# Where deferred steps are issued in a fused attention and MLP kernel: from a slot's due list to its late list

## The chip, the cores and the metric

The kernel runs on one core of one Trainium2 chip. A core has a matrix engine (PE, with its weight loads PEld), a vector engine (DVE), a scalar engine (ACT), a general engine (POOL) and a queue engine (SP) that issues the transfers. The metric is the device time of one execution in microseconds (us). The time before is 510.4 us, the median of three runs (510.28 to 510.7).

## The reference

The input is x of 2048 rows by 512. Everything is in 32-bit floats. `ln` is a layer norm without weights.

```python
qkv = ln(x) @ wqkv                      # 32 heads of 16
idx = pos[:, None] - 2 * arange(8)      # each row sees 8 rows, two apart, backwards
attn = softmax(where(idx >= 0, (q . k[idx]) * 16 ** -0.5, -1e9))
h   = x + (sum over the 8 of attn * v[idx]) @ wo
r   = max(ln(h) @ w1 + b1, 0)           # 1792 wide
out = h + (r * r) @ w2 + b2
```

## The kernel before, in words

Matrix products run on operands that are split in a high part, which the matrix engine's fast 32-bit format holds exactly, and a low part, the rest. Each product is the sum of three terms (high by high, low by high, high by low). In the code `hi` is the cast that makes the high part (ACT, L152) and `lo` the subtraction that makes the low part (L155, on DVE or POOL as the caller says). The matrix product of the attention result with `wo`, of the normalised rows with `w1` and of the squared relu with `w2` are all made so.

The 16 row tiles of 128 rows are worked on in four groups of four. A first phase does the projections to q, k and v, which go to HBM (`qkv_d`) and come back in windows. Then come three passes, u = 0, 1 and 2, and a last one in another form. A pass u does the MLP of group u and, beside it, the attention and the product with `wo` of group u + 1. The passes have 17 slots: in each, PE does one block of 128 of the first product (`mlp1`, tile `mm`), and three slots later that block's second product (`mlp2`, into four tiles `acc`). Two slots hold each a `wo` product (tile `wo`), put in by `wo_product`.

The other engines get their work from lists, in an order set by the code alone; each engine then runs its own queue in that order, and an instruction that waits holds all that stands behind it on its engine. `at(n, f)` puts a step on the due list of the slot n from now, `midway` on a middle list, `after` on a late list. A slot ends with `end_slot`, which first issues the due list, then moves the attention on with `pump`, then issues the middle list and the late list. So a step from the due list stands ahead of the attention steps of its slot on each engine, and one from the late list behind them.

`pump` draws from the stream `attention`: DVE makes the products of q and k (`pr`, L339), sums them (L373), takes maximum and difference (`mx` L390, `ex` L392), then ACT makes the exponential (`ex`, L396), DVE sums (`sm`, L362), normalises (L379, L367) and multiplies with v (`pr`, L350); POOL adds up these products in a triplet of additions to the attention result `o` (L407). ACT also copies q in (`qp`, L268). SP loads the windows k and v (L247) and q (L260) as their buffers come free of DVE's last use.

What the change touches:

- Attention result t is split into 16-bit halves by ACT (`o_split`: `pl<-o`, L616), turned by a transposing transfer on SP (`turn_dma`, L620), joined by ACT (`o_join`, L625), and cast to the two parts `oh`/`ol` or `ohl`, which the `wo` product reads. The same goes for normalised rows `hn`. The index i counts a group's four results; RI is 2.
- After a `wo` product come four steps: `h_add` (DVE, L661, with statistics L163 and L164, followed by three small steps `rs` of POOL), `h_norm` (ACT, `hn`, L196), `add_b2` (POOL, `h<-h,b_sb`, L674) and `spill` (SP to `h_d`, L677). `add_b2` prepares the row for the end of its own group's MLP.
- `split_w2` (u = 0 alone) makes the parts of one block of `w2` from `raw`: a cast into `big_h` or `w_x` at once, and a `lo` on the late list, on DVE for every third block and on POOL for the others. Low parts go to HBM (L1082) and are fetched in later passes (L1087).
- `hidden`, one slot after `mlp1`, makes relu and square on ACT (`r`, L871 and L872), the cast `rh` and, a slot later, the `lo` named `rl` on POOL.

The last pass works on pairs of blocks; POOL and DVE make sums of weights there (`traw`, L786 to L789), which ACT casts to `th` and a `lo` completes as `tl`.

Of the kernel before, what the change touches and what calls it, by code (L numbers as in the profile page):

```python
# [20 lines left out]
RI = 2  # L21
# [37 lines left out]
def block_kernel(ctx, tc, x, wqkv, wo, w1, b1, w2, b2, out):  # L59
# [53 lines left out]
    def at(delta, fn, *a):  # L113
        due.setdefault(now["slot"] + delta, []).append((fn, a))

    def after(delta, fn, *a):
        late.setdefault(now["slot"] + delta, []).append((fn, a))
# [4 lines left out]
    def end_slot(pe):  # L122
        now["pe"] += pe
        run(due)
        pump()
        run(amid)
        run(late)
        now["slot"] += 1

    def run(chores):  # L130
        todo = chores.get(now["slot"], [])
        while todo:
            fn, a = todo.pop(0)
            fn(*a)

    def dve(t):
        now["dve"] += t
# [80 lines left out]
    def mm3(ps, lh, ll, rh, rl, mid=None, at_=2 * KB, lows_last=False):  # L218


        terms = [[(l, r, k) for k in range(KB)] for l, r in ((lh, rh), (ll, rh), (lh, rl))]
        if lows_last:
            terms[1:] = terms[:0:-1]
        terms = sum(terms, [])
        for n, (l, r, k) in enumerate(terms):
            if mid and n == at_:
                mid()
            nc.tensor.matmul(ps, l(k), r(k), start=(n == 0), stop=(n == 3 * KB - 1))  # L228
# [454 lines left out]
    def wo_product(t, slots):  # L683
        ps = turn["mm"].tile("wo")
        oh, ol = oT.pop(t)
        mm3(ps, lambda k: oh[:, k, :], lambda k: ol[:, k, :],
            lambda k: wo_h[:, k, :], lambda k: wo_l[:, k, :], lows_last=t in OV)
        for n, (fn, a) in zip(slots, ((h_add, (t, ps)), (h_norm, (t,)), (add_b2, (t,)),
                                      (spill, (t,)))):
            (after if fn in (h_norm, spill) else at)(n + (fn is add_b2), fn, *a)  # L690

# [183 lines left out]
    def mlp1(u, f):  # L877
        ps = turn["mm"].tile("mm")
        fs = slice(f * P, (f + 1) * P)
        mm3(ps, lambda k: w1_h[:, k, fs], lambda k: w1_l[:, k, fs],  # L880
            lambda k: hh[k // 2][:, k % 2], lambda k: hl[k // 2][:, k % 2])
        at(1, hidden, u, f, ps)

    def mlp2(u, f, acc, js, first=False, last=False, mid=None):

        rh, rl = hid[u, f]
        terms = [(rh, w2_h, j) for j in js] + [(rh, w2_l, j) for j in js]
        if len(js) > 1:
            terms += [(rl, w2_h, j) for j in js]
        else:  # L890
            terms.insert(1, (rl, w2_h, js[0]))
        for n, (l, w, j) in enumerate(terms):
            if mid and n == len(terms) // 2:
                mid()
            nc.tensor.matmul(acc[j], l[:, j * P:(j + 1) * P], w[f],  # L895
                             start=(first and n < len(js)),
                             stop=(last and n >= len(terms) - len(js)))
# [79 lines left out]
    for n in range(16):  # L977
        gp, t = divmod(n, 4)
# [28 lines left out]
    def first_phase(t0):  # L1007
        def chores(m):
# [16 lines left out]
            for t in range(R):  # L1025
                if k == OT[t]:
                    at(0, load_h, t)
                    o_T(t)
                if t in HV and k == HK[t][0]:
                    at(0, h_split, t)  # L1030
                    after(0, turn_dma, ("h", t))
                if t in HV and k == HK[t][1]:
                    at(0, turn_join, ("h", t))
                if k == WO[t]:
                    wo_product(t, (1, 3, 4, 6))
                    now["pe"] += 2.73
                if k == HT[t]:
                    (at(0, h_parts, t) if t in HV else h_T(t))
# [12 lines left out]
    def load_w2(f):  # L1051
        raws[f] = row("raw2")
        nc.sync.dma_start(raws[f], w2[f * P:(f + 1) * P, :])
# [36 lines left out]
    for u in range(R - 1):  # L1090
        now["sub"] = u
        first, end = u == 0, False
        fs = list(range(FB)) if first else [*sorted(place), 12, 13]
        fs += [f for f in range(12) if f not in fs and (u < 2 or f not in ENDS)]
        fs += ENDS if u == 2 else []
        need = [] if first else [f for f in fs if f < 12 and f not in place]
        acc = [psum.tile([P, D], F32, name="acc", tag=tag) for tag in ("acc0", "acc1", "tr0", "tr1")]
        js = range(R)


        todo, halves = {}, {}
        for i in js:
            t = R * (u + 1) + i
            if not end:
                a = i // 2 if u == 2 else 0
                o0 = OP[i] - a - (2 if i >= RI and t in OV else 0)
                if t in OV:
                    turned = [(o0, at, 0, o_split, t), (o0, at if i >= RI else after, i // RI, turn_dma, ("o", t)),
                              (o0 + 2, at, 0, o_join, t)]
                else:  # L1110
                    turned = [(o0, o_T, t)]
                if t in HV:
                    h0 = 11 + i
                    turned += [(h0, midway, 0, h_split, t), (h0, after, 0, turn_dma, ("h", t)),
                               (h0 + 2, at, 0, turn_join, ("h", t))]
                for p, *what in ((LH[i] - a, at, 0, load_h, t), *turned,
                                 (WP[i] - a, wo_product, t, (0, 1, 2 + 3 * a, 3 + 3 * a))):
                    todo.setdefault(p, []).append(what)
                p, h = (HP[i], i % 2) if u < 2 else HL[i]
                if t in HV:  # L1120
                    todo.setdefault(p, []).append((at, 0, h_parts, t))
                else:
                    (todo, halves)[h].setdefault(p, []).append((h_T, t))
            todo.setdefault(UP[i], []).append((at, 0, unspill, R * u + i))
        if u == 2:
            for p, *what in ((12, at, 0, t_load, 0), (12, at, 0, t_load, 1), (13, after, 0, t_sums, 0),
                             (13, after, 0, t_sums, 1), (13, at, 1, t_split, 0),
                             (14, after, 0, t_split, 1)):
                todo.setdefault(p, []).append(what)

        def half(p):
            run(due)
            for fn, *a in halves[p]:
                fn(*a)

        for p in range(FB + LAG):
            more = 0.0
            if p == FB:
                run(due)
                dve(HOLD)  # L1140
            if u < 2 and p == FB - 2:
                dve(HOLD)
            for fn, *a in sorted(todo.get(p, []), key=lambda x: x[0] is wo_product):
                fn(*a)
                more += 2.73 if fn is wo_product else 0.0
            if p < FB:
                mlp1(u, fs[p])
                more += 2.73
                if first:
                    at(0, split_w2, p)  # L1150
                    if p + 1 < FB:
                        load_w2(p + 1)
            q = p - LAG
            if q >= 0:
                f = fs[q]
                mlp2(u, f, acc, js, q == 0, q == FB - 1,
                     (lambda: half(p)) if p in halves else None)
                more += 2.74
                if f < 12 and (need or first and p < FB - LAG):
                    free.append(place.pop(f))  # L1160
                    if need:
                        at(1, fetch, need.pop(0))
            end_slot(more)
        for i in js:
            at(u // 2, finish, R * u + i, acc[i])
# [83 lines left out]
```

## Time and profile before

| | |
|---|---|
| median of the runs | 510.4 us |
| the profiled execution | 510.82 us |
| its span | 509.0 us |
| PE busy | 498.7 us, 98% |
| DVE, POOL, ACT busy | 75%, 70%, 60% |
| granted clock of PE | 1.00 |

The span is the time between the first and the last recorded event of the profiled execution; the 1.8 us around it belong to its own time as well. A row of a timeline gives the start, the duration, the engine, the line, the operation, the tiles written and read (without their numbers), the shapes, how many instructions the row stands for, and in brackets how long the engine was idle before and whose event ended that. Matrix instructions overlap their neighbours, so that the distance between starts says more than the durations. In a row by stretches, each engine has its busy time and its count.

### The profile page before, as it was taken

To read this page: it belongs to the slowest core of one execution; us is meant where nothing else is said; L and a number is where in the kernel's file an instruction comes from. 1 tells how busy PE (TensorE), PEld (TensorE's weight loads), DVE (VectorE), ACT (ScalarE), POOL (GpSimd) and SP (SyncE) were. 2 spreads that over 40 slices of the span, in tenths; PEclk is the share of its full clock that TensorE was granted. 3 is DMA by queue.
4 is the path that set the end of the run, shared out by engine and by line. 5 is a ranking of instruction groups with operands and counts; after the bars stand their busy time and mean duration, and the time that the engine had idled before them with its cause. 6 is when DMAs were issued, how large, how long until landed. Compare 5 with 4: busy or idle time off the path is not lost.

```text
span 509.0 us, 7539 instructions
## 1 busy us (share of the span) xinstructions
PE 498.7 (98%) x2422; PEld 420.7 (83%) x2422; DVE 380.8 (75%) x512; ACT 304.7 (60%) x558; POOL 357.2 (70%) x434
## 2 busy tenths in 40 slices
PE   8999999999999999999999999989999999999997
PEld 7999778888888888887788888768888888998986
DVE  6469899999989799979879997898973137832233
ACT  4625677768346757386564566754556947566541
POOL 5714689986685899969777876976897465685610
PEclk9999999999999999999999999999999999999999
DMA  8577899989798898669676874967662372444212
GB/s 265 162 238 204 229 300 297 262 271 317 219 220 254 277 283 253 231 176 245 193 249 199 215 195 130 263 221 231 210 160 67 102 217 82 166 127 142 64 42 82
DMA packets 109359, 102.61 MB, mean 202 GB/s; under 512 B 29448, under 2 KB 77832, under 8 KB 109320
## 3 DMA queue, kind: packets, MB, share of 16 engines
q1 hardware_dynamic: 108376, 101.61, 68.0%
q10 hardware_dynamic: 944, 0.52, 0.3%
q8 instruction: 19, 0.31, 0.3%
q14 instruction: 20, 0.16, 0.1%
HBM read 72.65 MB, written 24.25 MB: 190 GB/s over the span
## 4 chain that ended last, share of the span: by engine, by line
PE 41%; POOL 5%; ACT 4%; DMA 3%; DVE 1%; issue 1%; SPq 0%; POOLq 0%; DVEq 0%; ACTq 0%
PE acc L895 19%; PE mm L228 12%; PE mm L818 6%; PE wo L228 3%; POOL pr L407 2%; DMA o<-pl 1%; DMA hn<-pl 1%; POOL h L674 1%; DMA h<-h_d 1%; ACT pl L625 1%; ACT pl L616 1%; ACT hn L196 1%; DVE pr L350 0%; POOL o L407 0%; PE tr L201 0%
## 5 line engine op out<-in xcount | busy, mean ns | idle before, releaser
L407 POOL TENSOR_TENSOR pr<-pr 128x512 f32<-128x512 f32 (+1 forms) x128 | 133.7, 1044 | 34.6 <-DVE pr L350 29.1
L228 PE MATMUL mm<-big_l,w_h 128*128 128x512 f32 x336 | 88.5, 390 | 1.6 <-DVE big_l L155 0.9
L350 DVE TENSOR_TENSOR pr<-ex,v 128x1024 f32<-128x1024 f32 x64 | 78.1, 1221 | 13.1 <-POOL o L407 8.1
L339 DVE TENSOR_TENSOR pr<-qp,k 128x1024 f32<-128x1024 f32 x64 | 76.8, 1200 | 8.8 <-ACT qp L268 6.9
L373 DVE TENSOR_REDUCE ex<-pr 128x64 f32<-128x1024 f32 x64 | 78.5, 1226 | 1.9
L228 PEld LDWEIGHTS mm<-big_l,w_h 128*128 128x128 f32 x336 | 62.9, 188 | 15.4 <-issue 1.3
L155 POOL TENSOR_TENSOR rl<-r,rh 128x512 fp32r<-128x512 f32 x42 | 55.5, 1322 | 20.2 <-ACT rh L152 20.2
L228 PE MATMUL mm<-big_l,xh 128*128 128x512 f32 (+1 forms) x208 | 55.8, 378 | 0.0
L228 PE MATMUL mm<-big_h,xh 128*128 128x512 f32 (+1 forms) x208 | 53.9, 380 | 1.3 <-ACT xh L152 1.0
L228 PE MATMUL mm<-big_h,xl 128*128 128x512 f32 (+1 forms) x208 | 52.7, 375 | 0.7 <-DVE xl L155 0.7
L895 PE MATMUL acc<-big_l,rh 128*128 128x512 f32 x190 | 52.2, 390 | 0.0
L895 PE MATMUL acc<-big_h,rh 128*128 128x512 f32 x190 | 52.1, 391 | 0.0
L895 PE MATMUL acc<-big_h,rl 128*128 128x512 f32 x190 | 51.7, 389 | 0.0
L228 PEld LDWEIGHTS mm<-big_h,xh 128*128 128x128 f32 x208 | 37.6, 188 | 8.9 <-ACT xh L152 2.6
L228 PE MATMUL mm<-big_l,w_l 128*128 128x512 f32 x168 | 44.9, 389 | 0.0
L228 PEld LDWEIGHTS mm<-big_h,xl 128*128 128x128 f32 x208 | 38.2, 188 | 6.9 <-DVE xl L155 1.1
L871 ACT ACTIVATE r<-mm,b_sb 128x512 f32<-128x512 f32 x42 | 28.7, 684 | 22.5 <-PE mm L228 20.7
L895 PEld LDWEIGHTS acc<-big_h,rl 128*128 128x128 f32 x190 | 35.7, 188 | 7.4
L895 PEld LDWEIGHTS acc<-big_l,rh 128*128 128x128 f32 x190 | 35.5, 188 | 7.4
L228 PEld LDWEIGHTS mm<-big_l,xh 128*128 128x128 f32 x208 | 37.5, 188 | 4.9
L895 PEld LDWEIGHTS acc<-big_h,rh 128*128 128x128 f32 x190 | 34.9, 188 | 6.7
L228 PEld LDWEIGHTS mm<-big_l,w_l 128*128 128x128 f32 x168 | 31.5, 188 | 6.6
(167 smaller groups left out, 918.7 us busy)
## 6 DMA issues: line engine op xcount, KB each, us to landing
k<-qkv_d SPq DMA_DIRECT2D x48, 288.0 KB, 3.0
v<-qkv_d SPq DMA_DIRECT2D x48, 288.0 KB, 4.1
qkv_d<-y SPq DMA_DIRECT2D x18, 512.0 KB, 4.7
big_l<-w2l_d SPq DMA_DIRECT2D x24, 256.0 KB, 3.0
xt<-in_A_x_dram SPq DMA_DIRECT2D x16, 256.0 KB, 4.2
q<-qkv_d SPq DMA_DIRECT2D x32, 128.0 KB, 3.8
h<-in_A_x_dram SPq DMA_DIRECT2D x16, 256.0 KB, 4.2
h_d<-h SPq DMA_DIRECT2D x16, 256.0 KB, 3.2
```

What stands on the lines that cost most here:

```text
L155: eng.tensor_tensor(out=dst, in0=src, in1=h, op=ALU.subtract)
L196: nc.scalar.activation(dst, src, AF.Identity, scale=rs[:, 0:1], bias=rs[:, 1:2])
L228: nc.tensor.matmul(ps, l(k), r(k), start=(n == 0), stop=(n == 3 * KB - 1))
L339: nc.vector.tensor_tensor(out=pr.rearrange("p i w h d -> p i w (h d)"), in0=qps["now"][:, j % 2].unsqueeze(2).to_broadcast([P, RI, W, GC]) ...
L350: nc.vector.tensor_tensor(out=p2, in1=vwin, op=ALU.mult, in0=e1[:, :, :, j * GH:(j + 1) * GH].unsqueeze(4).to_broadcast([P, RI, W, GH, DH]))
L373: nc.vector.tensor_reduce(out=lf[:, :, :, j * GH:(j + 1) * GH], in_=pr, axis=X, op=ALU.add)
L407: nc.gpsimd.tensor_tensor(out=dst, in0=p2[:, :, :w], in1=p2[:, :, w:2 * w], op=ALU.add)
L616: nc.scalar.copy(two_planes(planes[key][1]), halves_of(src))
L625: nc.scalar.copy(halves_of(pl).rearrange("p two n -> p n two"), two_planes(src).rearrange("p two n -> p n two"))
L818: nc.tensor.matmul(ps, sta[y][:, k], mov[x][:, k], start=(first and q == 0), stop=(last and q == len(terms) - 1), skip_group_check=True)
L871: nc.scalar.activation(r, ps, AF.Relu, bias=b1_sb[:, f:f + 1])
L895: nc.tensor.matmul(acc[j], l[:, j * P:(j + 1) * P], w[f], start=(first and n < len(js)), stop=(last and n >= len(terms) - len(js)))
```

## The change

Three sets of steps go from the due list to the late list of a slot. First, `add_b2` after every `wo` product: it keeps its slot, and stands in the list ahead of the `spill` of the same row. Second, `o_split` for the third result of a group (i equal to RI) in the passes u = 0 to 2; its `turn_dma`, which was on the due list of the next slot, is now on the late list of the same slot, behind the split. `o_join` stays two slots after the split. Third, `split_w2`: its cast and, in the list behind it, its `lo` (for POOL or DVE).

```diff
         for n, (fn, a) in zip(slots, ((h_add, (t, ps)), (h_norm, (t,)), (add_b2, (t,)),
                                       (spill, (t,)))):
-            (after if fn in (h_norm, spill) else at)(n + (fn is add_b2), fn, *a)
+            (at if fn is h_add else after)(n + (fn is add_b2), fn, *a)
...
                 if t in OV:
-                    turned = [(o0, at, 0, o_split, t), (o0, at if i >= RI else after, i // RI, turn_dma, ("o", t)),
+                    turned = [(o0, after if i == RI else at, 0, o_split, t),
+                              (o0, at if i > RI else after, i // (RI + 1), turn_dma, ("o", t)),
                               (o0 + 2, at, 0, o_join, t)]
...
                 if first:
-                    at(0, split_w2, p)
+                    after(0, split_w2, p)
```

The order of PE's instructions is the same before and after. The first place is ACT in the pass u = 0, at the slot of the third result's split (tile 6; `pl_2544` before, `pl_2575` after; `raw2_2434` is a block of `w2`). One piece of the difference:

```order
+L396 ACTIVATE ex_219<-ex_219 128x256
+L196 ACTIVATE hn_2573<-h_2093,rs_2462 128x512
+L616 COPY pl_2575<-o_2104 128x1024
 L152 CAST big_h_84<-raw2_2434 128x512
-L396 ACTIVATE ex_219<-ex_219 128x256
```

The split moves behind the exponential and the normalised row of tile 4, which stood behind it.

The second place is POOL in the same stretch. Before (the triplets on `pr` make the attention results; `h_2093` is the row of tile 4, `rl` are low parts of hidden blocks):

```order
L407 TENSOR_TENSOR pr_2482<-pr_2482 128x2x256
L407 TENSOR_TENSOR pr_2482<-pr_2482 128x2x128
L407 TENSOR_TENSOR o_2105<-pr_2482 128x2x64
L155 TENSOR_TENSOR rl_2532<-r_2530,rh_2531 128x512
L169 TENSOR_SCALAR rs_2549<-mv_2548 128x1
L171 TENSOR_TENSOR rs_2549<-rs_2549,mhalf_82 128x1
L172 TENSOR_SCALAR rs_2549<-mv_2548,rs_2549 128x1
L155 TENSOR_TENSOR rl_2607<-r_2605,rh_2606 128x512
L407 TENSOR_TENSOR pr_2619<-pr_2619 128x2x256
L407 TENSOR_TENSOR pr_2619<-pr_2619 128x2x128
L407 TENSOR_TENSOR o_2557<-pr_2619 128x2x64
L155 TENSOR_TENSOR big_l_85<-raw2_2516,big_h_84 128x512
```

And after:

```order
L155 TENSOR_TENSOR rl_2532<-r_2530,rh_2531 128x512
L407 TENSOR_TENSOR pr_2481<-pr_2481 128x2x256
L407 TENSOR_TENSOR pr_2481<-pr_2481 128x2x128
L407 TENSOR_TENSOR o_2104<-pr_2481 128x2x64
L169 TENSOR_SCALAR rs_2542<-mv_2541 128x1
L171 TENSOR_TENSOR rs_2542<-rs_2542,mhalf_82 128x1
L172 TENSOR_SCALAR rs_2542<-mv_2541,rs_2542 128x1
L155 TENSOR_TENSOR rl_2612<-r_2610,rh_2611 128x512
L407 TENSOR_TENSOR pr_2569<-pr_2569 128x2x256
L407 TENSOR_TENSOR pr_2569<-pr_2569 128x2x128
L407 TENSOR_TENSOR o_2554<-pr_2569 128x2x64
L155 TENSOR_TENSOR big_l_85<-raw2_2516,big_h_84 128x512
```

The low part `rl_2532` now stands ahead of the triplet that makes the third result. Right behind the rows shown stood, before, the addition of `h_2093` and then a low part `rl`; now the low part and a triplet stand ahead of that addition.

The third place is POOL at the beginning of the last pass, around the sums of weights. Before:

```order
L846 TENSOR_TENSOR r_4719<-u_4672,p_4671 128x256
L674 TENSOR_TENSOR h_4280<-h_4280,b2_sb_81 128x512
L786 TENSOR_TENSOR traw_4662<-traw_4662 128x2x128
L787 TENSOR_TENSOR traw_4662<-traw_4662 128x2x128
L788 TENSOR_TENSOR traw_4662<-traw_4662 128x2x128
L789 TENSOR_TENSOR traw_4662<-traw_4662 128x2x128
L674 TENSOR_TENSOR h_4343<-h_4343,b2_sb_81 128x512
L155 TENSOR_TENSOR tl_4803<-traw_4662,th_4802 128x512
```

And after:

```order
L846 TENSOR_TENSOR r_4719<-u_4672,p_4671 128x256
L786 TENSOR_TENSOR traw_4662<-traw_4662 128x2x128
L787 TENSOR_TENSOR traw_4662<-traw_4662 128x2x128
L788 TENSOR_TENSOR traw_4662<-traw_4662 128x2x128
L789 TENSOR_TENSOR traw_4662<-traw_4662 128x2x128
L674 TENSOR_TENSOR h_4280<-h_4280,b2_sb_81 128x512
L155 TENSOR_TENSOR tl_4802<-traw_4662,th_4801 128x512
L674 TENSOR_TENSOR h_4343<-h_4343,b2_sb_81 128x512
```

Both additions moved back, the one behind the sums, the other behind the low part `tl`.

## The prediction

> **What bounds the kernel now.** First the page: the busy time of each engine.
>
> ```profile
> PE 498.7 (98%) x2422; PEld 420.7 (83%) x2422; DVE 380.8 (75%) x512; ACT 304.7 (60%) x558; POOL 357.2 (70%) x434
> ```
>
> TensorE works in 498.7 of 509.0 us, and the order of its instructions does not change. The change can thus win only idle time of PE, or add some. So I asked second for the busy time by stretches of 20 us.
>
> ```profile
> 220.00:240.00 20.00, 19.31 (x85) 15.51 (x84) 18.99 (x20) 17.10 (x26) 15.24 (x16) 1.00 0.91 221
> 240.00:260.00 20.00, 19.32 (x89) 15.51 (x88) 17.20 (x29) 11.15 (x22) 13.84 (x17) 1.00 0.64 202
> 320.00:340.00 20.00, 19.02 (x84) 14.94 (x83) 17.36 (x24) 14.04 (x23) 16.96 (x22) 1.00 0.93 253
> ```
>
> The columns are span, then PE, PEld, DVE, ACT, POOL, the granted clock, the DMA share, GB/s. PE loses 0.69, 0.68 and 0.98 in these three; the clock is 1.00. Third, the timeline of PE at those places:
>
> ```profile
> 230.55 1.07 PE L228 MATMUL wo<-wo_h,ohl 128*128 128x512 f32 x4
> ...
> 232.36 1.17 PE L228 MATMUL wo<-wo_h,ohl 128*128 128x512 f32 x4
> 234.22 1.20 PE L228 MATMUL mm<-big_l,w_h 128*128 128x512 f32 x4 [0.69 <-ACT r L871]
> ...
> 247.06 1.07 PE L895 MATMUL acc<-w_x,rl 128*128 128x512 f32 x4
> 248.07 0.66 PE L201 MATMUL tr<-ident,hn 128*128 128x128 f32 x4
> 248.48 1.64 PE L895 MATMUL acc<-w_x,rh 128*128 128x512 f32 x6
> 250.81 0.66 PE L201 MATMUL tr<-ident,hn 128*128 128x128 f32 x4 [0.69 <-ACT hn L196]
> ...
> 321.39 1.20 PE L228 MATMUL wo<-wo_h,ohl 128*128 128x512 f32 x4 [0.54 <-ACT ohl L152]
> ...
> 332.25 1.20 PE L228 MATMUL wo<-wo_h,ol 128*128 128x512 f32 x4 [0.44 <-DVE ol L155]
> ...
> 343.47 1.15 PE L228 MATMUL mm<-big_l,w_h 128*128 128x512 f32 x4 [0.93 <-DVE big_l L155]
> ...
> 445.07 0.40 PE L818 MATMUL mm<-big_l,th 128*128 128x256 f32 x2
> 445.54 0.50 PE L818 MATMUL mm<-big_l,tl 128*128 128x256 f32 x2
> ```
>
> Two groups of four lie between 230.55 and 232.36, so four matmuls advance PE by 0.91, and the lost time is read from start to start: 234.22 less (232.36 + 0.91) is 0.95, and the group that follows a stop lasts 1.20 instead of 1.07, together 1.08. At 248.07 it is 248.07 less (247.06 + 0.91), 0.10; at 250.81 six matmuls after 248.48 end their share at 249.84, 0.97 lost. These three, 2.15, all lie in the first MLP group (u=0), behind the third attention result.
>
> **What makes PE wait there.** Fourth, the timelines of ACT, POOL, DVE and SP's queue in that stretch.
>
> ```profile
> 218.44 1.05 ACT L616 COPY pl<-o 128x1024 uint16<-128x1024 uint16 x1 [7.07 <-POOL o L407]
> ...
> 219.92 0.36 ACT L396 ACTIVATE ex<-ex 128x256 f32<-128x256 f32 x1
> 220.22 0.80 ACT L196 ACTIVATE hn<-h,rs 128x512 f32<-128x512 f32 x1
> 220.92 0.67 ACT L871 ACTIVATE r<-mm,b_sb 128x512 f32<-128x512 f32 x1
> ...
> 229.36 0.62 ACT L152 CAST ohl<-pl 128x512 fp32r<-128x512 f32 x1
> ...
> 230.75 1.05 ACT L616 COPY pl<-hn 128x1024 uint16<-128x1024 uint16 x1 [0.25 <-PE acc L895]
> 233.48 0.69 ACT L871 ACTIVATE r<-mm,b_sb 128x512 f32<-128x512 f32 x1 [1.69 <-POOL rl L155]
> ```
>
> ```profile
> 215.75 2.12 POOL L407 TENSOR_TENSOR pr<-pr 128x512 f32<-128x512 f32 x2
> ...
> 218.37 1.29 POOL L155 TENSOR_TENSOR rl<-r,rh 128x512 fp32r<-128x512 f32 x1
> ...
> 222.99 1.29 POOL L155 TENSOR_TENSOR rl<-r,rh 128x512 fp32r<-128x512 f32 x1 [2.00 <-ACT rh L152]
> 226.57 2.11 POOL L407 TENSOR_TENSOR pr<-pr 128x512 f32<-128x512 f32 x2 [2.29 <-DVE pr L350]
> ...
> 230.42 1.32 POOL L674 TENSOR_TENSOR h<-h,b_sb 128x512 f32<-128x512 f32 x1
> 231.67 1.78 POOL L155 TENSOR_TENSOR rl<-r,rh 128x512 fp32r<-128x512 f32 x1
> ```
>
> ```profile
> 214.43 0.69 DVE L661 TENSOR_TENSOR h<-wo,h 128x512 f32<-128x512 f32 x1 [0.42 <-PE wo L228]
> ...
> 220.31 0.42 DVE L362 TENSOR_REDUCE sm<-ex 128x32 f32<-128x256 f32 x1 [3.10 <-ACT ex L396]
> ...
> 223.25 1.58 DVE L155 TENSOR_TENSOR big_l<-raw,big_h 128x512 fp32r<-128x512 f32 x1
> ...
> 225.26 1.23 DVE L350 TENSOR_TENSOR pr<-ex,v 128x1024 f32<-128x1024 f32 x1
> ...
> 227.66 1.22 DVE L339 TENSOR_TENSOR pr<-qp,k 128x1024 f32<-128x1024 f32 x1
> ```
>
> ```profile
> 224.25 1.25 SPq L620 DMA_TRANSPOSE o<-pl  x1
> ```
>
> ACT stands 7.07 us, until 218.44, for the sum o of POOL, with the split pl at the head of its queue. Behind pl are the exponential ex, whose input DVE had finished long before, and hn. DVE therefore stands 3.10 us, its product pr (225.26 to 226.49) is late, POOL stands 2.29 for it, and POOL's queue after it (big_l, the bias addition, rl) ends only at 233.45: relu r waits 1.69 for that rl, and PE 0.69 for r.
>
> **The change part by part.** All three edits move issue places; no instruction is added or removed, so every cost is a shift in a queue.
>
> Split of the third result, u=0. ACT now runs ex and hn before pl. DVE does h first (214.43 + 0.69 + its statistics, to about 216), then the two small steps for ex (about 0.85), so ex can run at 216.9 and DVE goes on with sm at about 218.1, after one product, instead of 220.31: 2.2 earlier. The lo of second weights (223.25, 1.5 pitch) now stands behind the product pr instead of before it: 1.5 more. So pr ends near 222.7 instead of 226.49, and POOL's backlog begins some 3.8 earlier, limited by the rl that comes first (222.99 plus ACT's shift, below): about 2 earlier net. The bias addition (1.32) leaves its place ahead of rl. I get rl ended at about 229.9 instead of 233.45, so that r waits for ACT alone. The stop at 234.22 goes, and hn's two stops at 248.07 and 250.81, at the end of the same POOL queue, go with it: −2.15. Bounds: 0, if all is late again, and −2.15, all there is.
>
> What is late next: POOL does one rl (1.29) before the triplet that makes o, so o comes, and pl starts, at 219.7 instead of 218.44. pl's chain on ACT is 1.29 later and, without ex and hn in it (219.92 to 220.92), 1.00 shorter: +0.29. The cast ohl ended at 229.98, now 230.27; PE wants it at 230.55. It costs nothing, with 0.28 left. Then pl of hn (from 230.75, held by PE), the cast w_x, now behind it (a cast takes 0.62), and r would end near 233.0 against 233.27 where PE wants it. This cover is thin too, about 0.3.
>
> The transposing DMA at 224.25 is issued in the same slot as its split, but a v load now stands before it in SP's queue, which needs DVE's pr: 222.7 + its issue 0.4 is still before 224.25. Zero, as long as DVE's gain is over some 2 us.
>
> u=1. The same edit delays o there, and takes ex and hn out of the way between pl and the cast ohl on ACT:
>
> ```profile
> 310.10 0.37 ACT L396 ACTIVATE ex<-ex 128x256 f32<-128x256 f32 x1
> 310.41 0.80 ACT L196 ACTIVATE hn<-h,rs 128x512 f32<-128x512 f32 x1
> 311.11 0.61 ACT L182 ACTIVATE scrap<-h 128x512 f32<-128x512 f32 x1
> ```
>
> Plus 1.26 (one rl ahead of the triplet, or DVE's h with its statistics ahead of the product, which run side by side) and minus 1.01 (310.10 to 311.11): the stop at 321.39 grows by 0.25. The next one, 332.25, is set by the transposes and by ACT and DVE behind them, in an order that does not change, and not by PE, so it shrinks by the same 0.25. Net 0, between −1.9 (first rival) and +1.26.
>
> Bias additions. Four go to a slot's end, each 1.3 to 1.8 on POOL, behind an rl or behind sums. At the border to the last group I take two rows of ACT:
>
> ```profile
> 418.38 1.05 ACT L152 CAST th<-traw 128x1024 fp32r<-128x1024 f32 x1 [2.59 <-POOL traw L789]
> 419.98 0.69 ACT L871 ACTIVATE r<-mm,b_sb 128x512 f32<-128x512 f32 x1 [0.54 <-PE mm L228]
> ```
>
> An addition now stands before the sums traw, 1.3 later; th, waiting 2.59 for them, ends at 420.75 instead of 419.43, while r could begin at 419.98: ACT's chain shifts by 0.77 into the first products of the last group. I take +0.3 (ends 0 and +0.77; under the middle, since PE has a second product's work ahead of it and ACT has stood idle 0.54 and 2.59 in these two rows alone, so that part of the shift is caught up).
>
> In the last group an addition that stood before the next sums now comes after them; they are 1.3 earlier, and so is tl, which PE awaits at 445.54. It lost 0.23 (445.54 less 445.07 and the 0.24 that two of these matmuls take) and 0.10 (0.50 against 0.40): −0.33, between −0.33 and 0.
>
> The spill of a row to HBM now waits for a later addition; PE reads it back a whole group on. Zero; up to +0.3 if a transpose queued behind it on SP lands late.
>
> Splits of second weights (u=0, 14 of them). A cast (0.62) moves behind a q copy or an ex of 0.36 on ACT, and a lo one step back on DVE. Between 150 and 220 PE has no stop and the weight is read slots later: zero, ends −0.1 and +0.4 (one cast's delay, seen once).
>
> Sum against the profiled execution, 510.82 (span 509.0): 510.82 − 2.15 − 0.33 + 0.30 = 508.64. The median of the runs shown is 0.42 lower, so I forecast 508.2.
>
> **A rule weighed.** DVE's lo at 223.25 takes 1.58 beside POOL's rl (222.99 to 224.28), and the product at 227.66 takes 1.22 beside POOL's adds (226.57 to 228.68). In the Trainium skill, the page SBUF — State Buffer, section "SBUF: two separate sides", says that a DVE operation with two inputs in SBUF and a GpSimd operation share a port pair which the first takes for its whole instruction, while the other fully blocks. By that rule the trace agrees for the lo and not for the product, which ran through at 1.22. If it held for the products, the sum would be near 510.3 (third rival).
>
> **The rivals.**
>
> More gain. At u=1 the transpose goes out in its own slot, earlier on SP; if the next transposes land sooner, the stop at 332.25 (0.44, with restart 0.7) and the 0.93 after it at 343.47 go too: 508.2 − 0.7 − 1.1 = 506.4 (0.93 is 1.1 with its restart, as at 234.22). Against it: SP's queue there is full.
>
> Slower: the third result comes late. If DVE's pr stays near 226.49 (as when hn or ex on ACT is held by something else), the v load holds the transpose until 226.9, 2.65 after 224.25; ohl comes at 232.6 and PE loses 2.1 at 230.55, with the old stops still there. At u=1 pl is 1.26 late uncovered. 510.4 + 2.1 + 1.26 less what 332.25 absorbs (0.7) and 0.33 is 512.7. It decides once DVE gains under 2 us. For it: ACT's margins of 0.28. Against: DVE's 3.10 of idleness for ex is in the trace.
>
> No gain: the backlog is only shifted. DVE and POOL, both nearly full from 222 to 246, hold each other as at 223.25 (0.9 more each time); three such meetings use up the 2 us, and the stops at 234.22 and 250.81 return: 510.3.
>
> **How the numbers follow.** Forecast 0.44 (507.3 to 509.2); more gain 0.11 (506.4); no gain 0.19 (509.5 to 511.3); slower 0.26 (511.5 to 513.5). A change under 0.2%, 1.0 us, can hardly be told from none. Faster: 0.44 + 0.11 = 0.55; same 0.19; slower 0.26. The range 506.2 to 512.0 takes in the lower rivals and the milder half of the slower one.
>
> **What would show it.** Right: ex near 217 before pl, DVE without the 3.10, r at about 232.3 not waiting for rl, PE's busy time 19.9 or more from 220 to 260, no wait on hn L196. Wrong: a wait of PE for ohl at 230.55 above 0.3, the transpose issued after 225, a stop of PE between 431 and 440 above 0.5, or the old stops at the same place with other releasers.

## The result

The changed kernel takes 506.5 us (median of six runs, 505.79 to 508.76) against 510.34 us before (six runs of it on the same chip): the ratio is 0.9933, with a 95% interval of 0.9913 to 0.9952. It is 0.7% faster. The forecast was 508.2, so the direction was right and the time lies inside the range, but the gain is some 1.7 us larger than the likeliest case. A second set of six runs, shown further down, gives 507.35, so the median alone leaves the size of the gain open by almost 1 us; the profiles below narrow it.

The profiled execution of the changed kernel took 506.54 us, span 504.7. PE's busy time by stretches of 20 us:

```profile
220.00:240.00 20.00, 20.00 (x90) 16.57 (x89) 16.96 (x20) 17.67 (x28) 17.02 (x17) 1.00 0.95 242
240.00:260.00 20.00, 19.95 (x93) 16.26 (x92) 17.62 (x27) 11.65 (x22) 13.94 (x18) 1.00 0.69 223
...
300.00:320.00 20.00, 19.22 (x85) 15.60 (x84) 16.43 (x18) 13.49 (x22) 15.16 (x21) 1.00 0.72 192
320.00:340.00 20.00, 19.91 (x92) 16.06 (x91) 19.67 (x30) 12.10 (x23) 17.36 (x21) 1.00 0.75 230
```

The two stretches of the pass u = 0 are full, as forecast. One stop is left in u = 1, before 320; the stretch after it, which lost 0.98 before, loses 0.09. The timeline of PE, at the same instructions as those shown of before:

```profile
229.43 1.07 PE L228 MATMUL wo<-wo_h,ohl 128*128 128x512 f32 x4
...
232.15 1.07 PE L228 MATMUL mm<-big_l,w_h 128*128 128x512 f32 x4
...
246.11 1.64 PE L895 MATMUL acc<-w_x,rh 128*128 128x512 f32 x6
247.80 0.66 PE L201 MATMUL tr<-ident,hn 128*128 128x128 f32 x4
...
318.62 1.21 PE L228 MATMUL wo<-wo_h,ohl 128*128 128x512 f32 x4 [0.78 <-ACT ohl L152]
...
328.77 1.09 PE L228 MATMUL wo<-wo_h,ol 128*128 128x512 f32 x4
...
339.06 1.17 PE L228 MATMUL mm<-big_l,w_h 128*128 128x512 f32 x4
...
441.32 0.40 PE L818 MATMUL mm<-big_l,tl 128*128 128x256 f32 x2
```

PE's order is the same in both kernels, so I followed how far each matmul starts ahead of its place before, its lead, and read it in the quiet stretches between the stops. The lead grows by 1.09 at the former stop of 234.22 and by 0.80 at the two on hn (246.11 plus 1.36 for six matmuls is 247.47, so 0.33 of the second is left at 247.80). It shrinks by 0.26 at ohl of u = 1, grows by 0.82 at the former 332.25 and by 0.82 at 343.47, shrinks by 0.39 at the border to the last pass and grows by 0.33 at 445.54. That is 3.21 in all. The rest of the 4.3 between the spans lies in the first 67 us, where the two kernels run the same instructions in the same order:

```profile
63.83 1.20 PE L228 MATMUL mm<-big_h,xl 128*128 128x512 f32 x4 [0.77 <-DVE xl L155]
```

The same group of matmuls started at 65.01 in the profile of before, 1.18 later:

```profile
65.01 1.19 PE L228 MATMUL mm<-big_h,xl 128*128 128x512 f32 x4 [0.69 <-DVE xl L155]
```

Over all profiles of this study the group starts between 63.13 and 65.07, and no kernel changes anything before it. So I measure what an edit does by the time from the start of this group to the end of the span, the "rest" below: 443.99 before (509.0 less 65.01), 440.87 after, a gain of 3.1. Two profiles of one kernel agree within 0.1 in the rest (440.87 and 440.77; 439.26 and 439.30), but a single stop can vary by 0.3, as one of the kernels below shows.

Now the three engines behind PE in u = 0, after the change. ACT and DVE:

```profile
215.76 0.37 ACT L396 ACTIVATE ex<-ex 128x256 f32<-128x256 f32 x1 [4.99 <-DVE ex L392]
216.04 0.81 ACT L196 ACTIVATE hn<-h,rs 128x512 f32<-128x512 f32 x1
218.57 1.05 ACT L616 COPY pl<-o 128x1024 uint16<-128x1024 uint16 x1 [1.73 <-POOL o L407]
...
228.49 0.62 ACT L152 CAST ohl<-pl 128x512 fp32r<-128x512 f32 x1
```

```profile
216.76 0.41 DVE L362 TENSOR_REDUCE sm<-ex 128x32 f32<-128x256 f32 x1
...
220.20 1.22 DVE L350 TENSOR_TENSOR pr<-ex,v 128x1024 f32<-128x1024 f32 x1
```

With the lead of 1.12 that PE has here (230.55 less 229.43) added, ex runs at 216.9, pl starts at 219.7, ohl ends at 230.2 and pr at 222.5. DVE's 3.10 us of standing are gone. The low part rl that r had waited for ends at 229.9 (227.52 + 1.29 + 1.12), and r runs from 232.2 without a wait.

### The profile page after: what moved, and what is told of

Its sections match the earlier page's. It is cut to its first block, busy times and chain, and to the rows that moved or that the text cites. A ratio compares the mean times of both kernels' runs of the same rounds, so it can differ in the third digit from the quotient of the medians.

```text
span 504.7 us, 7544 instructions
## 1 busy us (share of the span) xinstructions
PE 497.3 (99%) x2422; PEld 421.1 (83%) x2422; DVE 380.5 (75%) x512; ACT 304.2 (60%) x558; POOL 356.4 (71%) x434
## 4 chain that ended last, share of the span: by engine, by line
PE 73%; POOL 5%; ACT 5%; DVE 3%; issue 2%; DMA 1%; SPq 0%; POOLq 0%; ACTq 0%
PE mm L228 35%; PE acc L895 23%; PE wo L228 7%; PE mm L818 6%; POOL pr L407 2%; PE tr L201 2%; ACT pl L616 1%; DVE pr L350 1%; DMA h<-h_d 1%; POOL o L407 1%; POOL rl L155 1%; ACT r L872 1%; POOL h L674 1%; ACT r L871 0%; ACT hn L196 0%
```

## Experiments

**Each edit alone.** The first kernel keeps only the second edit:

```diff
-                    turned = [(o0, at, 0, o_split, t), (o0, at if i >= RI else after, i // RI, turn_dma, ("o", t)),
+                    turned = [(o0, after if i == RI else at, 0, o_split, t),
+                              (o0, at if i > RI else after, i // (RI + 1), turn_dma, ("o", t)),
```

> Only the second edit: the third result's split and its transpose go to the late list in u = 0 to 2; bias additions and second weights stay as before. Theory S (the split at the head of ACT's queue held the exponential, and with it DVE's stream): nearly the whole gain comes from here, both stops after u = 1's wo product (0.71 and 0.94 us) and most of the 1.85 of u = 0, without the 0.32 lost at 435; the stop at ohl of u = 1 still grows by some 0.25. Time 506.3 to 507.8. Theory B (the bias additions ahead of rl on POOL were the cause): under 1 us of gain, 509.3 to 510.5.

It took 507.71 us (ratio 0.9951, interval 0.9932 to 0.997), the rest is 441.18: a gain of 2.8. By the lead: 1.09 and 1.05 in u = 0, minus 0.29 at ohl, 0.87 at 332.25, but only 0.18 at 343.47, where PE still waits:

```profile
340.36 1.16 PE L228 MATMUL mm<-big_l,w_h 128*128 128x512 f32 x4 [0.71 <-DVE big_l L155]
```

Theory S holds for the size; it was wrong that both stops of u = 1 go with the split. The second kernel has only the bias additions late:

```diff
-            (after if fn in (h_norm, spill) else at)(n + (fn is add_b2), fn, *a)
+            (at if fn is h_add else after)(n + (fn is add_b2), fn, *a)
```

> Only the first edit: the four bias additions of each pass go to the late list. Theory S: DVE keeps its 3.10 and 2.76 us of idleness for the exponential, the stops at 321, 332 and 343 stay. One thing can still be had: the addition of 1.32 us leaves its place ahead of the rl that ended at 233.45, so relu r begins about 1.2 earlier and the stop at 234.22 (1.0) goes, while PE loses 0.3 at the border to the last pass: 509.3 to 510.3. Theory B: 507.0 to 508.5, with the stops of u = 1 gone too.

510.57 us, ratio 1.0008 (0.9994 to 1.0023), the rest 444.23: no gain, 0.3 above the bounds given. The stop at 234.22 goes as expected (0.98), but 0.64 are lost just before it and 0.99 at hn, as the timeline of PE shows:

```profile
231.54 1.19 PE L228 MATMUL wo<-wo_h,ohl 128*128 128x512 f32 x4 [0.31 <-DVE ohl L155]
...
247.32 0.66 PE L201 MATMUL tr<-ident,hn 128*128 128x128 f32 x4 [0.93 <-ACT hn L196]
...
250.06 0.66 PE L201 MATMUL tr<-ident,hn 128*128 128x128 f32 x4 [0.69 <-ACT hn L196]
```

One of the additions, moved back in POOL's queue, now stands right ahead of the small steps for hn:

```profile
243.79 1.30 POOL L674 TENSOR_TENSOR h<-h,b_sb 128x512 f32<-128x512 f32 x1
245.17 0.22 POOL L169 TENSOR_SCALAR rs<-mv 128x1 f32<-128x1 f32 x1
```

Before, these steps followed the triplet directly. Counted from the group at 65 us, the first hn on ACT begins 0.69 later than before (246.45 less 63.57 against 247.20 less 65.01), and PE now waits 0.93 for it where it had no wait to speak of. The full change has an addition at this place too (POOL, 241.54), which is the likely reason that it wins 0.80 at hn where the split alone wins 1.05; no run isolates it. At 332.25 0.57 are won: DVE's ol, which PE awaits there, takes 0.68 instead of 1.04 and begins 0.19 earlier on the old clock. At the border to the last pass 0.39 are lost, and at 445.54 0.33 are won. Theory B falls. The third kernel has only the second weights late:

```diff
-                    at(0, split_w2, p)
+                    after(0, split_w2, p)
```

> Only the third edit: the splits of second weights go to the late list, in u = 0 alone. My prediction had it at zero by itself. But it also moves DVE's lo of 1.58 us behind the product pr that POOL waits for (225.26), which alone brings rl 1.5 earlier. If that holds, the stop at 234.22 goes here as well and part of that at 250.81: 508.4 to 509.6, and the edits overlap in u = 0. If DVE's lo is not what POOL waits for: 510.0 to 510.6. The stops of u = 1 stay in both cases.

509.02 us, ratio 0.9974 (0.9961 to 0.9987), the rest 442.57: a gain of 1.4, where the prediction had zero. DVE's lo is now behind the product and takes 0.68 instead of 1.58, and the product ends at 224.5 on the old clock instead of 226.49, although DVE still stands 2.60 for the exponential:

```profile
218.18 0.42 DVE L362 TENSOR_REDUCE sm<-ex 128x32 f32<-128x256 f32 x1 [2.60 <-ACT ex L396]
...
221.63 1.23 DVE L350 TENSOR_TENSOR pr<-ex,v 128x1024 f32<-128x1024 f32 x1
222.77 0.68 DVE L155 TENSOR_TENSOR big_l<-raw,big_h 128x512 fp32r<-128x512 f32 x1
```

The stops at 234.22 and on hn go (1.00 and 1.06 by the lead), and ohl of u = 0 costs 0.47 more. The split alone gains 2.8, the second weights alone 1.4, the bias additions alone minus 0.2; together they gain 3.1. So the edits overlap.

**The overlap in u = 0.** All three edits, but the split late in u = 1 alone:

```diff
-                    turned = [(o0, after if i == RI else at, 0, o_split, t),
-                              (o0, at if i > RI else after, i // (RI + 1), turn_dma, ("o", t)),
+                    turned = [(o0, after if i == RI and u == 1 else at, 0, o_split, t),
+                              (o0, at if i > RI or i == RI and u != 1 else after, 1 if i > RI or i == RI and u != 1 else 0, turn_dma, ("o", t)),
```

> All three edits, but the third result's split stays on the due list in u = 0 (its transpose as before there); it is late in u = 1 and 2. The split's own gain in u = 0 is 2.1 us (split alone), that of the second weights alone there 1.5. If the two remove the same stops once (POOL's late rl and hn), this kernel loses little against the full change: +0.3 to +0.8, 506.8 to 507.4. If the full change needs the split in u = 0: +1.5 to +2.1, 508.0 to 508.7. The stops of u = 1 are as in the full change.

(In the kernel that ran, the split is on the due list in u = 2 too.) 507.74 us, ratio 0.9946 (0.9925 to 0.9967); the rest is 441.16, 0.3 more than with the full change. The median is 0.3 above the first case's bounds, the rest is at their lower end: without the split in u = 0 the same stops go, and only ohl is late at the start of its product, by 0.57, of which 0.26 come back at hn (1.06 against 0.80). In u = 0 either the split or the second weights suffice for POOL's late rl and hn.

**The first stop of u = 1, 332.25.** My prediction left it as it was. The kernel before, with one transpose earlier on SP and nothing else:

```diff
-                    turned = [(o0, at, 0, o_split, t), (o0, at if i >= RI else after, i // RI, turn_dma, ("o", t)),
+                    turned = [(o0, at, 0, o_split, t),
+                              (o0, at, 0, turn_dma, ("o", t)) if i == RI and u == 1 else
+                              (o0, at if i >= RI else after, i // RI, turn_dma, ("o", t)),
```

> The kernel before with one move: in u = 1 the third result's transpose is issued right behind its split, ahead of four loads in SP's queue, so at about 310.3 instead of 315.6; ACT, DVE and POOL keep their orders. Theory D (the late transpose crowded the transfers behind it, and that made the stops at 332.25 and 343.47): these two shrink, 508.6 to 509.4. Theory S (these stops came from DVE's stream, which stood for the exponential): they stay, 510.0 to 510.6.

509.4 us, ratio 0.9984 (0.997 to 0.9998), the rest 443.31: a gain of 0.7. By the lead it is 0.86 at 332.25 and 0.20 at 343.47, almost the numbers of the split alone; 0.3 were lost in u = 0, ahead of the edit, so that much a stop varies between profiles. Theory D holds for the first stop. Most of the second stays, as theory S says, but the split alone, which frees DVE's stream, does not remove it either: neither theory explains it. Below, the last two transposes on SP's queue and the join of o on ACT, in the kernel before and in this one. Before:

```profile
319.48 1.24 SPq L620 DMA_TRANSPOSE hn<-pl  x1
320.77 3.46 SPq L620 DMA_TRANSPOSE o<-pl  x1
```

```profile
327.82 1.17 ACT L625 COPY pl<-o 128x1024 uint16<-128x1024 uint16 x1 [1.30 <-DMA o<-pl]
```

With the first transpose at 309.95:

```profile
318.86 1.36 SPq L620 DMA_TRANSPOSE hn<-pl  x1
320.26 2.14 SPq L620 DMA_TRANSPOSE o<-pl  x1
```

```profile
324.91 1.18 ACT L625 COPY pl<-o 128x1024 uint16<-128x1024 uint16 x1
```

The fourth result's transpose is issued 0.5 earlier, is through SP's queue 1.8 earlier (322.40 against 324.23; 0.3 of both is PE's lead), and ACT no longer waits for it. Behind the join ACT copies qp, DVE's product pr needs qp, and ol, which PE awaits at 332.25, stands behind pr on DVE. Before:

```profile
330.01 1.23 DVE L339 TENSOR_TENSOR pr<-qp,k 128x1024 f32<-128x1024 f32 x1 [2.00 <-ACT qp L268]
331.15 1.04 DVE L155 TENSOR_TENSOR ol<-pl,oh 128x512 fp32r<-128x512 f32 x1
```

With the first transpose at 309.95, DVE no longer stands for qp:

```profile
327.63 1.22 DVE L339 TENSOR_TENSOR pr<-qp,k 128x1024 f32<-128x1024 f32 x1
328.76 1.11 DVE L155 TENSOR_TENSOR ol<-pl,oh 128x512 fp32r<-128x512 f32 x1
```

The full change, by its trace, reaches this in another way: there the v load that stands ahead of the first transpose is released earlier, since DVE's stream no longer stands (transpose at 310.27 instead of 315.57, of which 3.0 is PE's lead), and the fourth result's transpose takes 2.30.

**The second stop of u = 1, 343.47.** PE waits there for four small lo of DVE. Their durations in the two kernels by tile (minimum, median, maximum in ns) differ. With the split alone, where the stop stays:

```profile
L155 DVE TENSOR_TENSOR big_l<-pl,big_l x4: 415/817/1509, 335.1 to 337.8; 128x256 fp32r<-128x256 f32 x4
```

With the full change, where it is gone:

```profile
L155 DVE TENSOR_TENSOR big_l<-pl,big_l x4: 415/419/1521, 334.6 to 335.6; 128x256 fp32r<-128x256 f32 x4
```

In the full change three of the four run at 0.42 and the last takes 1.52; with the split alone only the first runs at 0.42, and the others take 1.51, 0.96 and 0.68. I took the split alone and added two of the bias additions, those of u = 1:

```diff
-            (after if fn in (h_norm, spill) else at)(n + (fn is add_b2), fn, *a)
+            (after if fn in (h_norm, spill) or fn is add_b2 and t in (8, 9) else at)(
+                n + (fn is add_b2), fn, *a)
```

> The split alone, and of the bias additions only those of tiles 8 and 9 (u = 1) late. With the split alone the stop on big_l near 340 keeps 0.7 us of its 0.93, and the four lo of DVE there take 3.32 us beside POOL's triplet that starts 0.17 after them; in the full change they take 2.52, since POOL, which has an addition more ahead, starts its triplet 0.76 after them. Theory C (the meeting of DVE's lo with POOL's triplet decides, and the later additions move POOL): the stop is gone as in the full change, 0.7 less than the split alone, with the lo at 2.6 or less. Theory N (it comes from something else that the other edits do): the stop stays at 0.7 with the lo at 3.3.

506.94 us, ratio 0.9932 (0.9912 to 0.9951), the rest 440.80. The stop is gone (0.77 by the lead) and the four lo take 2.53:

```profile
334.52 2.53 DVE L155 TENSOR_TENSOR big_l<-pl,big_l 128x256 fp32r<-128x256 f32 x4
```

On POOL, one addition more stands ahead of the triplet, which begins at 335.28, after the lo have had their first go, while a small step before it is stretched from 0.27 to 0.78:

```profile
334.54 0.78 POOL L172 TENSOR_SCALAR rs<-mv,rs 128x1 f32<-128x1 f32 x1
335.28 2.37 POOL L407 TENSOR_TENSOR pr<-pr 128x512 f32<-128x512 f32 x2
```

With the split alone the triplet begins 0.17 after the lo (335.27 against 335.10) and the lo take 3.32. So these two additions gain 0.6 here (0.77 less 0.18). In the rest it is 0.4, since u = 0, which this edit does not touch, won 0.2 less in this profile. What they change beside the lo is where DVE and POOL meet. The experiment moved POOL's queue, not the meeting alone; that the meeting is the cause is argued from the durations.

**Two losses taken back.** In the full change ohl is late in u = 1 because a low part rl stands ahead of the triplet. It goes behind (the flag is set in slot 10 of u = 1):

```diff
-        at(0, lo, nc.vector if u == R - 1 else nc.gpsimd, rl, r, rh)
+        (after if now.get("rl") else at)(0, lo, nc.vector if u == R - 1 else nc.gpsimd, rl, r, rh)
...
+            now["rl"] = u == 1 and p == 10
```

> The full change, and in u = 1 the low part rl that stands ahead of the third result's triplet on POOL (303.44, 1.29 us) goes behind it. If that rl is the whole reason why ohl is late at 318.62 (0.78 of waiting, about 1.0 with the restart), ohl comes 1.25 earlier and this stop goes: 505.3 to 505.8. If ACT or DVE holds ohl for another reason, 506.2 to 506.8.

505.98 us, ratio 0.9909 (0.9882 to 0.9936), the rest 439.63: 1.2 better than the full change, and PE no longer waits for ohl. To this the next kernel adds the bias additions of tiles 12 and 13 on the due list:

```diff
-            (at if fn is h_add else after)(n + (fn is add_b2), fn, *a)
+            (at if fn is h_add or fn is add_b2 and t in (12, 13) else after)(
+                n + (fn is add_b2), fn, *a)
```

> As the kernel before this one, and the two bias additions of u = 2 (tiles 12 and 13) are back on the due list. The sums traw then start 1.3 us earlier and the 0.3 us lost near 431 should not be lost: 505.0 to 505.5, faster than both kernels. If the border to the last pass is late for another reason, no difference to the kernel before this one.

505.05 us, ratio 0.9898 (0.9861 to 0.9934), the rest 439.26. The 0.39 lost at the border to the last pass are back. In the full change PE loses part of them between these two groups, which start 0.46 apart:

```profile
430.58 0.40 PE L818 MATMUL mm<-big_l,w_h 128*128 128x256 f32 x2
431.04 0.51 PE L818 MATMUL mm<-wo_h,th 128*128 128x256 f32 x2
```

Here the same groups are 0.24 apart:

```profile
429.60 0.40 PE L819 MATMUL mm<-big_l,w_h 128*128 128x256 f32 x2
429.84 0.40 PE L819 MATMUL mm<-wo_h,th 128*128 128x256 f32 x2
```

The full change and this improved kernel once more, both on one chip:

> The full change once more, on one chip with the kernel that follows: 506.0 to 507.0, ratio to the kernel before 0.992 to 0.994.

> The full change with rl of u = 1 behind the third result's triplet and the bias additions of tiles 12 and 13 on the due list, repeated. By the traces two stops, 1.2 and 0.3 us, are gone against the full change: 1.2 to 1.8 us faster than it on the same chip.

The full change took 507.35 us (ratio 0.9932, 0.9911 to 0.9953), the improved one 505.61 (0.9899, 0.9879 to 0.9919): 1.7 between the medians, 1.5 between the rests (440.77 and 439.30). The first median is 0.35 above what was expected, which the first 65 us can make. The improved version is the fastest of the study; its four waits of PE that are left all lie in the start and the first phase:

```profile
PE tr L948 <- POOL ident masks.py:199: 1.3, 1, 1.3
PE mm L228 <- DVE xl L155: 1.0, 1, 1.0
PE mm L228 <- ACT xh L152: 0.7, 1, 0.7
PE tr L201 <- DVE xt L458: 0.3, 1, 0.3
```

## Why the prediction was right or wrong

**The sum.** Forecast were −2.15 in u = 0, 0 in u = 1 and +0.30 and −0.33 for the bias additions, −2.18 in all. By the lead it was −1.89, −1.38 (+0.26 at ohl, −0.82 and −0.82 at the two stops behind it), +0.39 and −0.33, −3.21 in all. So the miss of 1.0 is that of u = 1, reduced by 0.26 in u = 0 and by 0.09 at the border. Of the 3.84 between the medians 0.6 are not in the lead. The median of 506.5 lies below the likeliest case (507.3 to 509.2) and beside the rival "more gain" (506.4); that rival kept it in the range.

**The split in u = 0: right.** Mechanism and place hold, and nearly the size: ex before pl, DVE's standing gone, rl no longer ahead of r, the three stops are gone for 1.89 of the 2.15 forecast (0.33 of the last is left). The small numbers hold too: pl at 219.7 and ohl at 230.2 on the old clock, with 230.27 forecast, so the thin cover of 0.28 was enough.

**The sum's term for u = 1: wrong, and the main error.** "Net 0" has two parts. (Its lower bound is given as −1.9, while the rival that it names adds up to 0.7 and 1.1, 1.8.) The growth of the stop at ohl, 0.25 forecast, is 0.26, and its cause, the rl ahead of the triplet, is shown by the kernel that moves it. The step that failed is the sentence that 332.25 is set by an order that does not change and so only shrinks by PE's delay. The order did not change, but the start of the chain did: the first transpose leaves earlier, and one move of that transpose alone brings 0.86. This is the rival "more gain", which I had given 0.11; "against it: SP's queue there is full" was the wrong reading, since an earlier first transpose takes its load out of that stretch. The second stop, 343.47, I had tied to the same transposes. The bias additions of u = 1 remove it, which I had not forecast at all; that they do so by way of POOL's triplet and DVE's lo is argued from the durations.

**Bias additions: right at both priced places.** +0.30 was forecast at the border to the last pass; 0.39 was measured, and it is gone when the additions of tiles 12 and 13 go back. −0.33 was forecast at 445.54 and 0.33 won; with all additions on the due list it is not there (split alone: 0.00), and with only tiles 12 and 13 there it stays (0.33), so it belongs to the later ones. Their effect at 343.47 was missed, and so was the addition ahead of hn's small steps in u = 0.

**Second weights: wrong by themselves.** Costed at nothing, worth 1.4 alone. In the sum it did not matter, because I had counted DVE's lo (1.5) in the split's paragraph, and the two edits remove the same stops. That 1.5 was not needed: with the split alone the lo still stands ahead of the product, but takes 0.68 (at 220.62, with POOL's rl no longer beside it), and u = 0 wins 2.14.

**The rivals.** The slower one did not come: DVE gained 3.9 us on the old clock (pr at 222.5 instead of 226.49), above the 2 us from which it decides. "No gain" did not come either, and the prediction's reading of the rule that it hung on was wrong. In the Trainium skill, the page SBUF — State Buffer, section "SBUF: two separate sides", has a DVE operation with two inputs in SBUF and a GpSimd operation (POOL here) that reads SBUF block each other for a whole instruction. I took the product that ran through at 1.22 as a case against it, but that product has one input in SBUF: qp, and the ex of the other wide products, are tiles of the `psum` pool (L266, L283), where PE's results go, and not in SBUF. The traces agree with the rule: the four small lo, which read `pl` and `big_l` from SBUF, took 0.42 alone and up to 1.52 beside POOL's triplet; a lo of the same shape that reads `tr` of the `psum` pool took 0.41 to 0.43 and the wide products 1.16 to 1.23, in both profiles, beside POOL's additions or not. So what this rival feared of the wide products is not in these traces.

## What to carry to other kernels

An instruction that waits at the head of a queue delays what stands behind it, and here it paid to issue it after the work that does not wait; look for the engine that others wait for while it waits itself. A chain that keeps its order still moves when its first link is released earlier, so a stop that is "set by something else" must be followed to that first link before it is counted as fixed. When two edits clear the same backlog their gains do not add, and only runs of each alone show it.

## What was not expected of the hardware

Four lo of DVE, 0.42 us each alone, took 3.32 us where POOL's triplet began 0.17 us after them (before, and with the split alone) and 2.52 where it began 0.76 after them (the full change). Of this difference of 0.8, PE gained 0.6. The issue of one transpose on SP's queue lasted between 1.24 and 3.46 us, the longest right behind another transpose. And the first 65 us differ by almost 2 us between executions of kernels that are the same up to there.
